# Sliding-window attention: scores as whole 128x128 blocks in place of 32x64 tiles

## The chip, the cores and the metric

The kernel runs on one core of one Trainium2 chip. The metric is the device time of one execution in microseconds (us). The kernel before took 618.32 us as the median of 3 runs (617.77 to 619.11). In the tables and listings PE is TensorE's matmuls, PEld its weight loads, DVE is VectorE, ACT is ScalarE, POOL is GpSimd and SP is SyncE. L490 is line 490 of the kernel before.

## The reference

Two independent problems, A and B, are computed, and their outputs are put side by side. Each is attention with a causal window of 256 keys: S = 2048 tokens, D = 1024, 32 heads of 32, all in bf16.

```python
qkv = (x @ wqkv).reshape(B, S, 3, H, Dh)              # H = 32, Dh = 32
scores = einsum("bhqd,bhkd->bhqk", q, k) * Dh ** -0.5
mask = (idx[:, None] - idx[None, :] >= 0) & (idx[:, None] - idx[None, :] < 256)
scores = where(mask, scores, -1e9)
p = softmax(scores)
o = einsum("bhqk,bhkd->bhqd", p, v)
out = o.transpose(...).reshape(B, S, D) @ wo
```

With blocks of 128 tokens, a block j of keys meets the query blocks j (the diagonal, causal), j + 1 (all of it) and j + 2 (the far edge of the window).

## The kernel before

**Groups and stages.** Four heads make a head group: 4 x 32 = 128 rows. There are 8 groups per problem and 16 in all (G). Each group goes through projections of q and k (transposed, 128 rows by 2048 tokens), scores, exp, masks, accumulation with v, and a norm. v is projected for two groups at once (VG = 2), and the output projection of a problem follows when all its groups are through.

**Scores (`session`, L490 and L497).** Scores are laid out keys by queries. For a key block j the queries are cut in units of 64 (HALF): units 0 and 4 hold halves of the masked diagonal, 1 and 2 the middle block, 3 and 4 the far edge; unit 4 has the upper half of the keys at one end of the window and the lower half at the other. A matmul takes one head (32 rows) and 64 keys, so eight tiles of 32x64 lie beside each other in the array, four heads by two halves of keys. A session takes eight units (SLOTS), 8 x 64 = 512 columns of each of 4 heads, into one fixed tile of four PSUM banks, `scores`. One exp (L497) reads all 2048 columns of it to a bf16 tile `pt`. The 76 units of a group give 16 x 76 / 8 = 152 sessions. The next session's matmuls overwrite the tile, so they wait for the exp. The exp is not shifted by the row maximum; a range check over the inverse row sums (L585) guards it and chooses at the end between this path and a slow one.

**Masks (L507, L518).** GpSimd cuts the triangles out with affine selects of 64 columns: the diagonal goes into a tile `diag` of its own, the far edge is cut in place, 64 or 128 columns at once. Behind each select, `load_piece` may issue one piece of a later weight or x load: a memset of one column on GpSimd, which carries the wait for the buffer, and the DMA on SyncE's queue.

**Accumulation and norm (`edge`, `pv`).** A pair p of query blocks is accumulated PV_LAG = 2 sessions after its last scores. The 128x32 matmuls of L562 put p v into columns 0 to 255 of a PSUM bank `acc` and the row sums, by matmuls with ones, into columns 256 to 383. For the sums, `edge` adds the diagonal and the far block on VectorE first (L529), one session earlier. The norm on VectorE is a reciprocal of the sums (L575), two shuffles (L580), a multiply into `oT` (L582), and for every second pair the range check (L585). `acc` has two buffers, 16 x 8 = 128 pairs use them.

**Projections (`by_columns`, `evacuate`).** A chain is eight matmuls of 512 columns (or 16 of 256) into one of two PSUM banks `pp`, then one cast to bf16. In a session with an accumulation each of the matmuls is issued as four of 128x32 side by side (L199), in others as one of 128x128 (L195). The cast goes to ScalarE (L207) or VectorE (L209).

**What sets the order.** The kernel writes out the order of each engine's instructions by hand, session after session: scores and exp, selects with load pieces, the accumulations that are due, edge adds, then as many projection matmuls as `level` grants. `level` spreads the projections that may run, by the sessions at which their inputs land and at which their outputs are needed, over the sessions that are left, with at most NS_MOST ns each. `_Clock` keeps a running estimate of TensorE, ScalarE and VectorE from constants (COST, ACT_EXP, NS_*). By it `evacuate` picks the engine for a cast, and norms are handed out. An instruction that waits holds up all that stands behind it on its engine; TensorE's order is fixed too.

**Instructions.** Every matmul stands behind a weight load of its own. The program is unrolled, and each engine's instructions come to it by a DMA queue of their own (q8 is TensorE's in the profile).

Of the kernel before, what the change touches and what calls it, by code (L numbers as in the profile page):

```python
# [18 lines left out]
P = 128  # L19
# [7 lines left out]
SLOTS = 8  # L27
HALF = 64
PT_BUFS = 5
DG_BUFS = 4  # L30
VG = 2
NS_MM = 216.0
NS_ROW = 450.0
NS_PV = 52.0
NS_MOST = 3900.0
PV_LAG = 2
# [44 lines left out]
def _fast_path(ctx, tc, cfg, problems, outs, consts, certify):  # L81
# [11 lines left out]
    units = [(j, i) for j in range(NB) for i in range(5)  # L93
             if i in (0, 4) or j + (i + 1) // 2 < NB]
    NE = len(units)
    order = {e: n for n, e in enumerate(units)}
    END = -(-G * NE // SLOTS)

    def parts(j, q):
        return [(j, i) for i in {0: (4, 0), 1: (1, 2), 2: (3, 4)}[q - j]]  # L100

    entries = [(j, q) for j in range(NB) for q in range(j, min(j + 3, NB))]

    def place(g, u):
        return divmod(g * NE + order[u], SLOTS)

    def when(g, j, q, pick=max):
        return pick(place(g, u)[0] for u in parts(j, q))
# [4 lines left out]
    def first_use(g, k, of):  # L113
        return min(when(g, *e, min) for e in entries if e[of] // QB == k)

    def runs(g, us):
        out = []
        for n, u in enumerate(us):
            t, a = place(g, u)
            if out and out[-1][0] == t and out[-1][1] + out[-1][2] == a:  # L120
                out[-1][2] += 1
            else:
                out.append([t, a, 1, n])
        return out
# [8 lines left out]
    ptp = ctx.enter_context(tc.tile_pool(name="pt", bufs=PT_BUFS))  # L133
    diagp = ctx.enter_context(tc.tile_pool(name="diag", bufs=DG_BUFS))
# [9 lines left out]
    edges, diags = {}, {}  # L144
# [149 lines left out]
    def pv_time(g, p):  # L294
        return max(when(g, *e) for e in entries if e[1] // 2 == p) + PV_LAG

# [42 lines left out]
    def units_of(now):  # L339
        return [(n // NE,) + units[n % NE]  # L340
                for n in range(now * SLOTS, min((now + 1) * SLOTS, G * NE))]

    def far_runs(us):
        out = []
        for a, (g, j, i) in enumerate(us):
            if i > 2 and j + 2 < NB:
                if out and i == 4 and out[-1][0] == a - 1:
                    out[-1][1] = 2
                else:
                    out.append([a, 1])  # L350
        return out
# [5 lines left out]
    for time, key, fs in wanted:  # L357
        free = max(free, time)
        new = fs[0]
        for where, f in fs[1:]:  # L360
            while len(pieces.get(free, [])) >= min(2 if key[0] == "x" else 4,
                                                   len(far_runs(units_of(free)))
                                                   + sum(i in (0, 4) for _, _, i in units_of(free))):
                free += 1
            pieces.setdefault(free, []).append((new, where, f))
            new = None
        arrival[key] = free + (3 if key[0] in ("x", "wv") else 2)
# [96 lines left out]

    def session(now):
        us = units_of(now)
        n = len(us)
        clock.pe = max(clock.pe, clock.exp) + NS_ROW
        todo = []
        a = 0  # L470
        while a < n:
            b = a
            while b < n and us[b][:2] == us[a][:2]:
                b += 1
            g, j, _ = us[a]
            lo = [x for x in range(a, b) if us[x][2] < 4]
            hi = [x for x in range(a, b) if us[x][2] < 4 or j + 2 < NB]
            if lo:
                todo.append((g, j, 0, lo[0], len(lo), j * P + HALF * (us[lo[0]][2] + 1)))
            if hi:  # L480
                todo.append((g, j, 1, hi[0], len(hi), j * P + HALF * (us[hi[0]][2] + 1)))
            if us[b - 1][2] == 4:
                todo.append((g, j, 0, b - 1, 1, j * P))
            a = b
        for g, j, c, a, w_, q in todo:
            qT, kT = qks[g]
            keys = slice(j * P + c * HALF, j * P + (c + 1) * HALF)
            for r in range(4):
                rows = slice(32 * r, 32 * r + 32)
                nc.tensor.matmul(  # L490
                    scores[c * HALF:(c + 1) * HALF, r, a * HALF:(a + w_) * HALF],
                    lhsT=kT[rows, keys], rhs=qT[rows, q:q + w_ * HALF],
                    start=True, stop=True, tile_position=(32 * r, c * HALF),
                    skip_group_check=True)
        pt = ptp.tile([P, 4, SLOTS * HALF], BF16, name="pt")
        pts[now] = pt
        nc.scalar.activation(out=pt[:, :, :n * HALF], in_=scores[:, :, :n * HALF],  # L497
                             func=ACT.Exp, bias=-SHIFT, scale=cfg.scale)
        clock.act = max(clock.act, clock.pe) + ACT_EXP
        clock.exp = clock.act  # L500

        def diag(g, j, i):
            p, h = divmod(j, 2)
            if (g, p) not in diags:
                diags[(g, p)] = diagp.tile([P, 4, 2, P], BF16, name="diag")
            lo = HALF if i == 0 else 0
            nc.gpsimd.affine_select(out=diags[(g, p)][:, :, h, lo:lo + HALF],  # L507
                                    in_=pt[:, :, a * HALF:(a + 1) * HALF],
                                    pattern=[[0, 4], [1, HALF]], compare_op=ALU.is_ge, fill=0.0,
                                    base=lo, channel_multiplier=-1)  # L510
            load_piece(now)

        for a, (g, j, i) in enumerate(us):
            if i in (0, 4):
                diag(g, j, i)
        for a, w_ in far_runs(us):
            blk = pt[:, :, a * HALF:(a + w_) * HALF]
            nc.gpsimd.affine_select(out=blk, in_=blk, pattern=[[0, 4], [-1, w_ * HALF]],  # L518
                                    compare_op=ALU.is_gt, fill=0.0,
                                    base=-HALF * (us[a][2] - 3), channel_multiplier=1)  # L520
            load_piece(now)

    def edge(g, p):
        both = edgep.tile([P, 4, 2, P], BF16, name="both")
        dg = diags[(g, p)]
        todo = [(h, n * HALF, w_ * HALF, t, a * HALF) for h in range(2)
                for t, a, w_, n in runs(g, parts(2 * p + h - 2, 2 * p + h))]
        for h, o, w_, t, a in todo:
            nc.vector.tensor_tensor(out=both[:, :, h, o:o + w_], in0=dg[:, :, h, o:o + w_],  # L529
                                    in1=pts[t][:, :, a:a + w_], op=ALU.add)  # L530
            clock.dve = max(clock.dve, clock.pe) + COST["edge"] * (1.0 if w_ == P else 0.65)
        edges[(g, p)] = both

    def pv(g, p):
# [3 lines left out]
        dg = diags.pop((g, p))  # L538

        def old(us):  # L540
            return [(n * HALF, w_ * HALF, pts[s_][:, :, a * HALF:(a + w_) * HALF])
                    for s_, a, w_, n in runs(g, us)]

        mids = [old(parts(q - 1, q)) if q else [] for q in (2 * p, 2 * p + 1)]
        moves = []
        if p:
            moves += [(None, 2 * p - 2) + x for x in old(parts(2 * p - 2, 2 * p))]
            moves += [(None, 2 * p - 1) + x
                      for x in old(parts(2 * p - 1, 2 * p) + parts(2 * p - 1, 2 * p + 1))]
        moves += [(None, 2 * p, P + o, w_, src) for o, w_, src in mids[1]]  # L550
        moves += [(None, 2 * p + i, i * P, P, dg[:, :, i, :]) for i in range(2)]
        for i in range(2):
            moves += [(i, 0, 2 * P + o, w_, src) for o, w_, src in mids[i]]
        acc = ps_acc.tile([P, 512], F32, name="acc")
        clock.pe = max(clock.pe, clock.norms.pop(0))
        sums = edges.pop((g, p)) if p else dg
        moves += [(i, 0, 2 * P, P, sums[:, :, i, :]) for i in range(2)]
        for x, (h, j, o, w_, src) in enumerate(moves):
            for r in range(4):
                c = u * P + 32 * r  # L560
                lhsT = vts[(m, j // QB)][:, j % QB, c:c + 32] if h is None else ones[:, h, :]
                nc.tensor.matmul(acc[32 * r:32 * r + 32, o:o + w_], lhsT=lhsT,  # L562
                                 rhs=src[:, r, :], start=(x == 0), stop=(x == len(moves) - 1),
                                 tile_position=(0, 32 * r), skip_group_check=True)
            clock.pe += NS_PV * w_ / P
# [62 lines left out]
    flips.append(ps_st.tile([P, 4, SLOTS * HALF], F32, name="st")[:, 0])  # L628
# [31 lines left out]
    scores = ps_st.tile([P, 4, SLOTS * HALF], F32, name="st")  # L660
# [241 lines left out]
```

## Time and profile before

The profiled execution took 617.77 us, and its span from first to last recorded instruction is 616.0 us, at a granted TensorE clock of 0.999.

| engine | busy us | share of the span | instructions |
|---|---|---|---|
| PE | 598.9 | 97% | 16665 |
| PEld | 372.8 | 61% | 16665 |
| DVE | 429.9 | 70% | 1143 |
| ACT | 405.8 | 66% | 372 |
| POOL | 372.1 | 60% | 918 |

| group | count | busy us | mean ns of one |
|---|---|---|---|
| L497 exp | 152 | 285.5 | 1878 |
| L207 casts on ACT (512 columns) | 213 | 124.5 | 585 |
| L209 casts on DVE | 42 | 28.3 | 664 to 685 |
| L575 reciprocal | 128 | 121.9 | 953 |
| L529 edge adds | 256 | 144.8 | 602 |
| L580 shuffles | 256 | 64.5 | 297 |
| L582 multiply | 128 | 54.4 | 425 |
| L507 diagonal selects, 64 columns | 512 | 216.3 | 448 |
| L518 far selects | 256 | 161.0 | 647 |

A matmul's own duration is longer than its share of TensorE, since matmuls overlap: what one costs is the distance from its start to the next one's start. Groups whose instructions overlap have a busy time below count times mean. The first scores start at 15.8 us, the last session's at 561.6 us, and from 570.9 us on TensorE runs output projections alone. The DMA engines are busy 80 to 90% of the time in the first two of 40 slices and mostly 0 to 40% later.

### The profile page before, as it was taken

Reading aid. Unit: us, or ns where it says so; the run is one execution under the profiler, and the core shown is the slowest. Engines: PE = TensorE matmul, PEld = TensorE weight load, DVE = VectorE, ACT = ScalarE, POOL = GpSimd, SP = SyncE. Lnnn points to the kernel's source line nnn. Section 1 sums busy time; section 2 is a strip of 40 time slices with the busy share of each in tenths; the row PEclk is TensorE's granted clock in tenths of the full one; section 3 lists DMA queues with packets and bytes.
Section 4 is the critical chain, followed back from the end, with each engine's and each line's share of the span. In section 5 each row is a group of like instructions: output and inputs, shape, how many; then the busy total and the mean of one; then the engine's idle time right before and its main releaser. Section 6 shows DMA issues by size and latency. Waiting matters only on the chain.

```text
span 616.0 us, 36878 instructions
## 1 busy us (share of the span) xinstructions
PE 598.9 (97%) x16665; PEld 372.8 (61%) x16665; DVE 429.9 (70%) x1143; ACT 405.8 (66%) x372; POOL 372.1 (60%) x918
## 2 busy tenths in 40 slices
PE   8999999999999899999999999999999999999996
PEld 4666577657665666656565766756555765555443
DVE  1388878777877678776887757777878778788200
ACT  3667766877776668666676666667766767665332
POOL 0476767776766667675766667566666766665000
PEclk9999999999999999999999999999999999999999
DMA  9814110111024410346011010112021040114221
GB/s 234 176 47 133 37 39 5 39 37 39 5 46 76 95 38 4 67 104 123 29 38 39 4 39 4 39 37 64 29 53 40 5 106 12 56 55 131 70 78 64
DMA packets 86836, 36.00 MB, mean 58 GB/s; under 512 B 65552, under 2 KB 86160, under 8 KB 86672
## 3 DMA queue, kind: packets, MB, share of 16 engines
q1 hardware_dynamic: 85632, 33.31, 22.4%
q8 instruction: 132, 2.16, 1.5%
q10 hardware_dynamic: 1040, 0.26, 0.2%
q14 instruction: 32, 0.26, 0.2%
HBM read 17.83 MB, written 8.39 MB: 43 GB/s over the span
## 4 chain that ended last, share of the span: by engine, by line
PE 90%; issue 3%; POOL 2%; DMA 2%; DVE 1%; ACT 1%; SPq 0%; POOLq 0%; ACTq 0%
PE pp L199 46%; PE pp L195 22%; PE acc L562 13%; PE st L490 9%; DMA xT<-in_A_x_dram 2%; POOL diag L507 1%; POOL pt L518 1%; DVE both L529 0%; DVE rinv L575 0%; ACT pt L497 0%; SPq L603 0%; DVE wide L580 0%; ACT osb L207 0%; DVE top L585 0%; ACT vt L207 0%
## 5 line engine op out<-in xcount | busy, mean ns | idle before, releaser
L497 ACT ACTIVATE pt<-st 128x2048 bf16<-128x2048 f32 x152 | 285.5, 1878 | 90.2 <-PE st L490 63.1
L507 POOL TENSOR_SCALAR_AFFINE_SELECT diag<-pt 128x256 bf16<-128x256 bf16 x512 | 216.3, 448 | 194.3 <-ACT pt L497 180.5
L199 PE MATMUL pp<-xT,wqk 128*32 128x512 bf16 x3092 | 185.9, 379 | 0.4 <-issue 0.4
L575 DVE RECIPROCAL rinv<-acc 128x128 f32<-128x128 f32 x128 | 121.9, 953 | 62.1 <-PE acc L562 61.4
L518 POOL TENSOR_SCALAR_AFFINE_SELECT pt<-pt 128x512 bf16<-128x512 bf16 (+1 forms) x256 | 161.0, 647 | 0.0
L529 DVE TENSOR_TENSOR both<-diag,pt 128x512 bf16<-128x512 bf16 (+1 forms) x256 | 144.8, 602 | 15.1 <-POOL diag L507 11.1
L199 PEld LDWEIGHTS <-wqk 128*32 128x32 bf16 x3092 | 83.1, 97 | 63.3 <-issue 2.0
L199 PE MATMUL pp<-wv,xT 128*32 128x256 bf16 x2840 | 88.4, 273 | 0.5 <-issue 0.5
L199 PEld LDWEIGHTS <-xT 128*32 128x32 bf16 x2840 | 75.5, 97 | 6.6 <-issue 1.1
L490 PEld LDWEIGHTS <-kT 32*64 32x64 bf16 x3904 | 41.1, 103 | 57.6 <-issue 57.4
L490 PE MATMUL st<-qT,kT 32*64 32x64 bf16 (+4 forms) x3904 | 66.3, 236 | 2.3 <-issue 2.2
L580 DVE STREAM_SHUFFLE wide<-rinv 128x128 f32<-128x128 f32 x256 | 64.5, 297 | 0.0
L207 ACT CAST osb<-pp 128x512 bf16<-128x512 f32 (+1 forms) x58 | 33.5, 578 | 46.6 <-PE pp L195 29.3
L195 PE MATMUL pp<-xT,wqk 128*128 128x512 bf16 (+1 forms) x267 | 58.8, 367 | 1.1 <-DMA xT<-in_A_x_dram 1.1
L195 PE MATMUL pp<-wo_sb,oT 128*128 128x512 bf16 (+1 forms) x269 | 58.2, 373 | 0.4 <-ACT vt L207 0.3
L199 PE MATMUL pp<-wo_sb,oT 128*32 128x512 bf16 x1004 | 58.5, 379 | 0.0
L582 DVE TENSOR_TENSOR oT<-acc,wide 128x256 bf16<-128x256 f32 x128 | 54.4, 425 | 4.4
L562 PE MATMUL acc<-pt,vt 128*32 128x128 bf16 (+2 forms) x1792 | 50.8, 224 | 1.5 <-issue 1.4
L562 PEld LDWEIGHTS <-vt 128*32 128x32 bf16 x2816 | 42.4, 96 | 15.8 <-issue 5.2
L207 ACT CAST vt<-pp 128x512 bf16<-128x512 f32 x53 | 30.9, 584 | 20.4 <-PE pp L199 14.1
L207 ACT CAST qT<-pp 128x512 bf16<-128x512 f32 x51 | 29.8, 585 | 21.5 <-PE pp L199 13.8
L195 PEld LDWEIGHTS <-oT 128*128 128x128 bf16 x269 | 25.8, 98 | 29.8 <-issue 0.8
(47 smaller groups left out, 397.3 us busy)
## 6 DMA issues: line engine op xcount, KB each, us to landing
out_dram<-osb SPq DMA_DIRECT2D x63, 128.0 KB, 1.8
wqk<-in_B_wqkv_dram SPq DMA_DIRECT2D x32, 128.0 KB, 3.0
wqk<-in_A_wqkv_dram SPq DMA_DIRECT2D x24, 128.0 KB, 3.5
wo_sb<-in_A_wo_dram SPq DMA_DIRECT2D x16, 128.0 KB, 2.9
wv<-in_B_wqkv_dram SPq DMA_DIRECT2D x16, 128.0 KB, 2.9
wo_sb<-in_B_wo_dram SPq DMA_DIRECT2D x16, 128.0 KB, 2.6
oT<-in_A_x_dram SPq DMA_DIRECT2D x4, 256.0 KB, 5.0
wv<-in_A_wqkv_dram SPq DMA_DIRECT2D x2, 512.0 KB, 4.5
```

What stands on the lines that cost most here:

```text
L195: nc.tensor.matmul(out[:, lo:hi], lhsT=lhsT, rhs=rhs, start=start, stop=stop, skip_group_check=True)
L199: nc.tensor.matmul(out[c:c + 32, lo:hi], lhsT=lhsT[:, c:c + 32], rhs=rhs, start=start, stop=stop, tile_position=(0, c), skip_group_check=True)
L207: nc.scalar.copy(out=out, in_=in_)
L490: nc.tensor.matmul(scores[c * HALF:(c + 1) * HALF, r, a * HALF:(a + w_) * HALF], lhsT=kT[rows, keys], rhs=qT[rows, q:q + w_ * HALF], start ...
L497: nc.scalar.activation(out=pt[:, :, :n * HALF], in_=scores[:, :, :n * HALF], func=ACT.Exp, bias=-SHIFT, scale=cfg.scale)
L507: nc.gpsimd.affine_select(out=diags[(g, p)][:, :, h, lo:lo + HALF], in_=pt[:, :, a * HALF:(a + 1) * HALF], pattern=[[0, 4], [1, HALF]], co ...
L518: nc.gpsimd.affine_select(out=blk, in_=blk, pattern=[[0, 4], [-1, w_ * HALF]], compare_op=ALU.is_gt, fill=0.0, base=-HALF * (us[a][2] - 3) ...
L529: nc.vector.tensor_tensor(out=both[:, :, h, o:o + w_], in0=dg[:, :, h, o:o + w_], in1=pts[t][:, :, a:a + w_], op=ALU.add)
L562: nc.tensor.matmul(acc[32 * r:32 * r + 32, o:o + w_], lhsT=lhsT, rhs=src[:, r, :], start=(x == 0), stop=(x == len(moves) - 1), tile_positi ...
L575: nc.vector.reciprocal(out=inverses[0][:, turn % 2, :], in_=acc[:, 2 * P:3 * P])
L580: nc.vector.stream_shuffle(out=wide[:, h * P:(h + 1) * P], in_=inverses[0][:, turn % 2, :], mask=[16 * h] * 32)
L582: nc.vector.tensor_tensor(out=oTs[(pi, k)][:, t, (p % 2) * 256:(p % 2 + 1) * 256], in0=acc[:, 0:256], in1=wide[:], op=ALU.mult)
```

## The change

Scores are computed for whole blocks of 128 keys by 128 queries with 32x128 tiles (four heads side by side). A session has four such blocks (SLOTS = 4), 45 blocks per group in place of 76 units. The PSUM tile `st` is taken anew from its one-buffer pool in each session. The masks are cut in place in `pt`, one select of 128 columns for a diagonal and one for a far block, and the `diag` tiles are gone. `pt` has 7 buffers instead of 5, and an accumulation follows 3 sessions after its last scores instead of 2. The edge adds and accumulations take whole blocks. The planner's constants change with it (NS_ROW 420, NS_MOST 3300). The range check at L585, which the change's name speaks of, is the same in both kernels.

```diff
-SLOTS = 8
-HALF = 64
-PT_BUFS = 5
-DG_BUFS = 4
+SLOTS = 4
-NS_ROW = 450.0
+NS_ROW = 420.0
-NS_MOST = 3900.0
-PV_LAG = 2
+NS_MOST = 3300.0
+PV_LAG = 3
...
-    units = [(j, i) for j in range(NB) for i in range(5)
-             if i in (0, 4) or j + (i + 1) // 2 < NB]
-    NE = len(units)
+    entries = [(j, q) for j in range(NB) for q in range(j, min(j + 3, NB))]
+    NE = len(entries)
...
-    ptp = ctx.enter_context(tc.tile_pool(name="pt", bufs=PT_BUFS))
-    diagp = ctx.enter_context(tc.tile_pool(name="diag", bufs=DG_BUFS))
+    ptp = ctx.enter_context(tc.tile_pool(name="pt", bufs=7))
...
-        for g, j, c, a, w_, q in todo:
-            qT, kT = qks[g]
-            keys = slice(j * P + c * HALF, j * P + (c + 1) * HALF)
-            for r in range(4):
-                rows = slice(32 * r, 32 * r + 32)
-                nc.tensor.matmul(
-                    scores[c * HALF:(c + 1) * HALF, r, a * HALF:(a + w_) * HALF],
-                    lhsT=kT[rows, keys], rhs=qT[rows, q:q + w_ * HALF],
-                    start=True, stop=True, tile_position=(32 * r, c * HALF),
-                    skip_group_check=True)
+            g, j, q = es[a]
+            qT, kT = qks[g]
+            for r in range(4):
+                nc.tensor.matmul(
+                    st[:, r, a:b, :],
+                    lhsT=kT[32 * r:32 * r + 32, j * P:(j + 1) * P],
+                    rhs=qT[32 * r:32 * r + 32, q * P:(q + b - a) * P],
+                    start=True, stop=True, tile_position=(32 * r, 0))
...
+        for a, (g, j, q) in enumerate(es):
+            blk = pt[:, :, a, :]
+            if q == j:
+                nc.gpsimd.affine_select(out=blk, in_=blk, pattern=[[0, 4], [1, P]],
+                                        compare_op=ALU.is_ge, fill=0.0, base=0,
+                                        channel_multiplier=-1)
+            elif q == j + 2:
+                nc.gpsimd.affine_select(out=blk, in_=blk, pattern=[[0, 4], [-1, P]],
+                                        compare_op=ALU.is_gt, fill=0.0, base=0,
+                                        channel_multiplier=1)
+            if q != j + 1:
+                load_piece(now)
...
+        for h in range(2):
+            (s0, a0), (s1, a1) = (place(g, 2 * p + h - d, 2 * p + h) for d in (0, 2))
+            nc.vector.tensor_tensor(out=both[:, :, h, :], in0=pts[s0][:, :, a0, :],
+                                    in1=pts[s1][:, :, a1, :], op=ALU.add)
+            clock.dve = max(clock.dve, clock.pe) + COST["edge"]
...
-    scores = ps_st.tile([P, 4, SLOTS * HALF], F32, name="st")
```

More of the change, by code (lines that the diff above doesn't have):

```diff
@@ L91, in _fast_path, with place @@
     clock = _Clock()
-    units = [(j, i) for j in range(NB) for i in range(5)
-             if i in (0, 4) or j + (i + 1) // 2 < NB]
-    NE = len(units)
-    order = {e: n for n, e in enumerate(units)}
+    entries = [(j, q) for j in range(NB) for q in range(j, min(j + 3, NB))]
+    NE = len(entries)
+    order = {e: n for n, e in enumerate(entries)}
     END = -(-G * NE // SLOTS)
[L99 to L108, printed above, removed]
+    def place(g, j, q):
+        return divmod(g * NE + order[(j, q)], SLOTS)
     def begin(g):
@@ L113, in first_use @@
     def first_use(g, k, of):
[L114 to L124, printed above, removed]
+        return min(place(g, *e)[0] for e in entries if e[of] // QB == k)
     xpool = ctx.enter_context(tc.tile_pool(name="xT", bufs=NQ + 2))
@@ L143, in _fast_path @@
     xT, wqk, wv, wo_sb, vts, oTs, qks, pts = {}, {}, {}, {}, {}, {}, {}, {}
-    edges, diags = {}, {}
+    edges = {}
     inverses = [None]
@@ L294, in pv_time @@
     def pv_time(g, p):
-        return max(when(g, *e) for e in entries if e[1] // 2 == p) + PV_LAG
+        return max(place(g, *e)[0] for e in entries if e[1] // 2 == p) + PV_LAG
     def wv_time(m):
@@ L337, in _fast_path, with entries_of @@
     wanted.sort(key=lambda w: w[0])
-    def units_of(now):
-        return [(n // NE,) + units[n % NE]
+    def entries_of(now):
+        return [(n // NE,) + entries[n % NE]
                 for n in range(now * SLOTS, min((now + 1) * SLOTS, G * NE))]
[L343 to L351, printed above, removed]
     pieces = {}
@@ L360, in _fast_path @@
         for where, f in fs[1:]:
-            while len(pieces.get(free, [])) >= min(2 if key[0] == "x" else 4,
-                                                   len(far_runs(units_of(free)))
-                                                   + sum(i in (0, 4) for _, _, i in units_of(free))):
+            while len(pieces.get(free, [])) >= min(2 if key[0] == "x" else SLOTS, sum(
+                    q != j + 1 for _, j, q in entries_of(free))):
                 free += 1
@@ L465, in session @@
     def session(now):
-        us = units_of(now)
-        n = len(us)
+        es = entries_of(now)
+        n = len(es)
+        st = ps_st.tile([P, 4, SLOTS, P], F32, name="st")
         clock.pe = max(clock.pe, clock.exp) + NS_ROW
-        todo = []
         a = 0
@@ L472, in session @@
             b = a
-            while b < n and us[b][:2] == us[a][:2]:
+            while b < n and es[b][:2] == es[a][:2]:
                 b += 1
[L475 to L483, printed above, removed]
-            a = b
-        for g, j, c, a, w_, q in todo:
-            qT, kT = qks[g]
-            keys = slice(j * P + c * HALF, j * P + (c + 1) * HALF)
-            for r in range(4):
-                rows = slice(32 * r, 32 * r + 32)
-                nc.tensor.matmul(
-                    scores[c * HALF:(c + 1) * HALF, r, a * HALF:(a + w_) * HALF],
-                    lhsT=kT[rows, keys], rhs=qT[rows, q:q + w_ * HALF],
-                    start=True, stop=True, tile_position=(32 * r, c * HALF),
-                    skip_group_check=True)
-        pt = ptp.tile([P, 4, SLOTS * HALF], BF16, name="pt")
+            g, j, q = es[a]
[6 more added lines that the diff above has]
+                    start=True, stop=True, tile_position=(32 * r, 0))
+            a = b
+        pt = ptp.tile([P, 4, SLOTS, P], BF16, name="pt")
         pts[now] = pt
-        nc.scalar.activation(out=pt[:, :, :n * HALF], in_=scores[:, :, :n * HALF],
+        nc.scalar.activation(out=pt[:, :, :n, :].rearrange("p r a q -> p r (a q)"),
+                             in_=st[:, :, :n, :].rearrange("p r a q -> p r (a q)"),
                              func=ACT.Exp, bias=-SHIFT, scale=cfg.scale)
@@ L500, in session @@
         clock.exp = clock.act
[L502 to L521, printed above, removed]
+        for a, (g, j, q) in enumerate(es):
[10 more added lines that the diff above has]
+                load_piece(now)
@@ L523, in edge @@
     def edge(g, p):
         both = edgep.tile([P, 4, 2, P], BF16, name="both")
[L525 to L531, printed above, removed]
+        for h in range(2):
[3 more added lines that the diff above has]
+            clock.dve = max(clock.dve, clock.pe) + COST["edge"]
@@ L537, in pv @@
         k, h = divmod(p, QB // 2)
[L538 to L553, printed above, removed]
+        segs = []
+        for j in range(max(2 * p - 2, 0), 2 * p + 2):
+            for q in range(max(j, 2 * p), min(j + 3, 2 * p + 2)):
+                s, a = place(g, j, q)
+                if segs and segs[-1][0] == j and segs[-1][2] == s:
+                    segs[-1][4] += 1
+                else:
+                    segs.append([j, q, s, a, 1])
         acc = ps_acc.tile([P, 512], F32, name="acc")
         clock.pe = max(clock.pe, clock.norms.pop(0))
-        sums = edges.pop((g, p)) if p else dg
-        moves += [(i, 0, 2 * P, P, sums[:, :, i, :]) for i in range(2)]
+        moves = [(None, j, (q - 2 * p) * P, n * P, pts[s][:, :, a:a + n, :])
+                 for (j, q, s, a, n) in segs]
+        for (j, q, s, a, n) in segs:
+            for i in range(n):
+                if p == 0 or q + i == j + 1:
+                    moves.append((q + i - 2 * p, j, 2 * P, P, pts[s][:, :, a + i:a + i + 1, :]))
+        if p:
+            both = edges.pop((g, p))
+            moves += [(h, 0, 2 * P, P, both[:, :, h:h + 1, :]) for h in range(2)]
         for x, (h, j, o, w_, src) in enumerate(moves):
@@ L562, in pv @@
                 nc.tensor.matmul(acc[32 * r:32 * r + 32, o:o + w_], lhsT=lhsT,
-                                 rhs=src[:, r, :], start=(x == 0), stop=(x == len(moves) - 1),
+                                 rhs=src[:, r, :, :], start=(x == 0), stop=(x == len(moves) - 1),
                                  tile_position=(0, 32 * r), skip_group_check=True)
@@ L627, in _fast_path @@
     flips = [f[:] for f in flips]
-    flips.append(ps_st.tile([P, 4, SLOTS * HALF], F32, name="st")[:, 0])
+    flips.append(ps_st.tile([P, 4, SLOTS, P], F32, name="st")[:, 0].rearrange("p a q -> p (a q)"))
     flips.append(None)
```

## The prediction

> **What bounds the kernel now.** I read the page first (busy times, queues, chain), then the timeline of TensorE, then the packet records of the instruction queue, and last the groups with shapes kept apart.
>
> ```profile
> span 616.0 us, 36878 instructions
> ...
> PE 598.9 (97%) x16665; PEld 372.8 (61%) x16665; DVE 429.9 (70%) x1143; ACT 405.8 (66%) x372; POOL 372.1 (60%) x918
> ...
> q8 instruction: 132, 2.16, 1.5%
> ...
> PE 90%; issue 3%; POOL 2%; DMA 2%; DVE 1%; ACT 1%; SPq 0%; POOLq 0%; ACTq 0%
> ```
>
> TensorE is busy for 97% and holds 90% of the chain, so the time is TensorE's work plus what TensorE waits for. The "issue" share (3%, in the finer listing 2.6%, 16 us) is waiting for nothing that the profile shows. The timeline shows how such a wait looks:
>
> ```profile
> 207.68 0.43 PE L199 MATMUL pp<-xT,wqk 128*32 128x512 bf16 x4
> 208.04 0.42 PE L490 MATMUL st<-qT,kT 32*64 32x256 bf16 x20
> 208.39 0.40 PE L562 MATMUL acc<-pt,vt 128*32 128x128 bf16 x12
> 208.62 0.28 PE L562 MATMUL acc<-diag,vt 128*32 128x128 bf16 x8
> 208.74 0.28 PE L562 MATMUL acc<-pt,ones 128*32 128x128 bf16 x6
> 209.86 0.23 PE L562 MATMUL acc<-pt,ones 128*32 128x128 bf16 x2 [0.85 <-issue]
> ```
>
> The gap before 209.86 stands in the middle of one accumulation, six matmuls of a group of eight before it and two behind it, where no data can be late. The packet records say what is late: the instruction queue (q8) moves blocks of 16 KB (2.16 MB / 132), and 33,330 TensorE records over some 130 blocks are 256 instructions each. Of the 17 gaps over 0.38 us between 15 and 600 us, 16 stand at the same place of a block (instruction 184 to 190 modulo 256), and each ends 1.2 to 1.6 us after a fetch's packet has ended (206.72 + 1.75 = 208.46, TensorE goes on at 209.86). So TensorE stalls when it runs through a block before the next one is there. The shortest distances between two fetches are 3.2 to 3.5 us: a block that is used up faster than about 3.4 to 3.5 us makes TensorE wait for the rest.
>
> The same start times give the pitches: a 512-column group 216 ns, 256 columns 109, 128 columns 56, 64 columns 29, whether as one 128x128 matmul or four 128x32. Into scores there are 309 instead of 216 ns, so 93 for the change of tile shape. The scores of a session then take 0.35 us to the next line's first matmul (208.04 to 208.39; median 357 ns). A session costs 450 ns. (The planner's constant for it, NS_ROW, is 450 and agrees; the new one is 420.) Adding pitches session by session gives the measured start-to-start within 18 ns each, except in 30 sessions that are 16 us longer together: about 13 us are instruction fetches (below I use 12, the middle of what the block rule gives), some 3 us are waits for projection banks.
>
> **The change, part by part.** The title speaks of a range check, but both kernels read it from the row sums (64 operations at L585, 523 ns, the last line below): that part is nothing. What changes is the score tiling and all that hangs on it.
>
> ```profile
> L497 ACT ACTIVATE pt<-st 128x2048 bf16<-128x2048 f32 x152 | 285.5, 1878 | 90.2 <-PE st L490 63.1 <-issue 10.9 <-PE acc L562 6.6
> ...
> L518 POOL TENSOR_SCALAR_AFFINE_SELECT pt<-pt 128x512 bf16<-128x512 bf16 x192 | 132.0, 698 | 0.0
> L575 DVE RECIPROCAL rinv<-acc 128x128 f32<-128x128 f32 x128 | 121.9, 953 | 62.1 <-PE acc L562 61.4
> L529 DVE TENSOR_TENSOR both<-diag,pt 128x512 bf16<-128x512 bf16 x192 | 113.9, 616 | 14.9 <-POOL diag L507 11.1 <-POOL wqk L377 1.2 <-POOL pt L518 1.1
> ...
> L585 DVE SCALAR_TENSOR_TENSOR top<-rinv,top 128x256 int32<-128x256 int32 x64 | 33.5, 523 | 0.0
> ```
>
> *Scores, +6.7 us.* A head group has 45 blocks of 128x128 in place of 76 units of 64 queries, so 16 groups make 720 / 4 = 180 sessions, not 1216 / 8 = 152. A session streams 512 columns in two or three groups of four 32x128 matmuls, which the trace of before doesn't show. Price: 93 in, about 217 for the columns (163 + 56 or 109 + 109), and 107 out (a 128-column score group to the next line takes 164, a 256-column one 211, against 56 and 109): 417 ns. 180 x 0.417 - 152 x 0.450 = 75.1 - 68.4 = +6.7. Bounds: 400 ns if the wider columns drain faster (-3.1 us from that), 450 ns, the session before, if they cost no less (+5.9). I take 417, next to the constant 420.
>
> *Accumulation, -0.5 us.* By the listed order: 960 groups of 128 columns, 80 of 256, 192 of 64 become 856 of 128 and 180 of 256: 68.0 to 67.6 us. With the 18 ns of 28 more sessions, +0.5, the two cancel.
>
> *Instruction fetch, -10.5 us.* Score matmuls go from 3904 to 1488, accumulating ones from 4928 to 4144, and all matmuls from 16,665 to some 12,840, each with its weight load: 130 blocks become 100. Scores and accumulation together are 132 instructions in 0.95 us before and 81 in 0.95 us after; behind them a projection of 256-column groups, eight instructions in 109 ns, needs 2.4 us for the remaining 175. So the densest block takes about 3.4 us, where it took 2.6. Summing what each block lacks to 3.4 and 3.5 us gives 10.0 and 13.2 us for before, 1.0 and 1.6 us for after. I take 12 to 1.5; bounds 0 and 4 us left.
>
> The Trainium skill (Runtime: NRT & Kernel Launch, section Instruction fetch mechanics) says that the sequencer fetches the next page of 256 instructions while it runs the current one, and that crossing a boundary is mostly hidden. This trace agrees on the size of a block and not on the hiding. By the rule this term would be 0, and the change would come out at 630.8 us.
>
> *Queues of ACT and VectorE, +5.8 us.* 28 more exps of 1.878 us put 53 us on ACT. The planner answers by giving VectorE 79 of the 257 casts instead of 42 (ACT 178 for 215). In the first half the sessions shrink from 3.3 to 2.8 us (planned work divided over more of them). There VectorE has per accumulation 0.95 (reciprocal) + 1.08 (0.875 pairs of edge adds of 616) + 0.50 (two shuffles, 64.5 us over 128) + 0.43 (multiply) + 0.26 (half a range check), and 40 casts for 64 accumulations x 0.67 = 0.42: 3.6 us every 3.98 us, 91%, where 60 to 270 us shows 78%:
>
> ```profile
> 60.00:270.00 210.00, 203.99 (x6362) 134.20 (x6354) 164.28 (x443) 151.09 (x134) 145.64 (x365) 1.00 0.20 42
> ```
>
> Behind a late VectorE stand a cast whose projection bank TensorE needs two chains later (1.73 us per chain), and the norm that frees one of two acc banks. I laid the listed order out with these rows: each exp 0.5 us behind its score start, casts (0.59, 0.67) and norms in their places, TensorE waiting for the bank or the acc two back. For before it gives 3.2 us of waits (the trace leaves 3); for after 9.0, 5.9 for projection banks and 3.0 for acc, the latter between sessions 27 and 81. The exps themselves still fit: 0.56 + 1.88 of 2.8 us. Bounds: 0 more, and twice, +12.
>
> *At nothing.* GpSimd: 768 selects become 480 of 698 ns, 377 to 335 us; VectorE waits 11 us for it in all, and those edge adds are due two sessions later. The 144 load pieces hang on fewer selects and still have two or three sessions, 2 x 2.97 = 5.9 us against landings of 2.6 to 3.5. Without that cover a chain would wait for wqk or wv, a microsecond for each one that a piece is late. At the start x chunk 3 lands at 28.9 us, session 5 begins at 15.8 + 5 x 2.81 = 29.9: 1 us of cover. No queue gets a new DMA. PV_LAG of 3 sessions with 7 pt buffers is 8.9 us for masks and edges, against 7.0 for 2.
>
> **Sum.** +6.7 - 0.5 + 0.5 - 10.5 + 5.8 = +2.0 us on the span of 616.0. The profiled run took 617.77 for that span, the median is 618.32; I add to the median: **620.3 us**. Its own range is 617.5 to 624.
>
> **Rivals.** *The queues hold*: VectorE's backlog stays below the two-bank reserve, since the planner has counted it, and the fetches decide: 620.3 - 5.8 = 614.5 us. For it: ACT and VectorE wait 63 and 61 us for TensorE, and no exp delayed TensorE (the shortest time from an exp's end to the next scores is 0.70 us). Against it: 5% of the chains before already start within 0.05 us of their bank coming free. It decides once the added waits stay under some 2.5 us. *Fetches wait on traffic, not on density*: the fetch at 206.7 took 1.75 us beside the x transposes. Then each fetch costs as before, 12 x 100 / 130 = 9.2 us stay, and 620.3 + 7.7 = 628.0 us, the slower end. Against it: the wait at 393.4 followed a fetch of 0.99 us. *Weight loads of 32x128 show*: one of 98 ns (the 128x128 load) per session, 180 x 0.098 = +17.6, 638 us; but the 32x64 loads of 101 ns follow each other at 3 ns.
>
> **Numbers.** Chances: forecast 0.47, queues hold 0.33, traffic 0.13, weight loads 0.04, the rest 0.03 for a late load. Two runs of this kernel can't be told apart within 0.2%, 1.24 us: faster is below 617.1, slower above 619.6. The rival at 614.5 and a little of the forecast's lower edge give 0.35 faster; most of the forecast and the last three give 0.50 slower; 0.15 between. The range goes from 612 (queues hold and a 400 ns session) to 628.
>
> **What would show it.** Right: 100 q8 blocks and hardly a gap inside an accumulation; scores to next line 0.32 us; VectorE at 85% or more between 60 and 270 us, with TensorE waiting there for casts and for acc. Wrong: gaps at one place of the block as before; sessions far from 417 ns; an even step of 2.8 us in the first half without waits, which is 614.5; or exps that start late and hold the next scores, which I price at 0.1 us.

## The result and the profile after

The changed kernel took 611.24 us (611.07 to 611.60, 4 runs), the kernel before 618.72 us (617.77 to 621.31, 4 runs): a ratio of 0.9873, 95% interval 0.9843 to 0.9904. It is faster where slower was forecast, and it lies 0.8 us below the range. The page of after, with the lines that answer to those shown of before:

```profile
span 609.6 us, 28777 instructions
...
PE 599.8 (98%) x12838; PEld 345.0 (57%) x12838; DVE 437.3 (72%) x1148; ACT 434.8 (71%) x363; POOL 317.8 (52%) x630
...
q8 instruction: 102, 1.67, 1.2%
...
PE 73%; DVE 3%; issue 1%; ACT 1%; DVEq 0%; ACTq 0%
...
L452 ACT ACTIVATE pt<-st 128x2048 bf16<-128x2048 f32 x180 | 338.0, 1878 | 100.0 <-PE st L444 81.3
```

TensorE has 3,827 matmuls fewer: 2,416 of scores, 784 of accumulations and 627 of projections, since fewer of these go as four of 128x32. 102 blocks of instructions are fetched instead of 132. ACT has its 28 more exps at the same 1878 ns. The chain of after can be followed back to 126 us only, so its shares don't compare with those of before. TensorE's own list of waits does (who waited for whom: us in total, times, longest us). Before:

```profile
PE acc L562 <- issue: 4.9, 10, 1.1
PE st L490 <- issue: 2.2, 3, 1.4
PE pp L199 <- issue: 0.9, 2, 0.5
```

After, no line of TensorE's matmuls names issue any more; the longest of those that are left, but for one of 1.3 us at the start that both kernels have, are:

```profile
PE pp L172 <- ACT qT L184: 0.8, 3, 0.4
PE acc L506 <- DVE oT L526: 0.7, 1, 0.7
```

Next TensorE's timeline over one session with an accumulation (start, duration, instruction, count):

```profile
312.28 0.39 PE L176 MATMUL pp<-xT,wqk 128*32 128x512 bf16 x4
312.60 0.40 PE L444 MATMUL st<-qT,kT 32*128 32x384 bf16 x8
312.93 0.51 PE L506 MATMUL acc<-pt,vt 128*32 128x128 bf16 x16
313.27 0.28 PE L506 MATMUL acc<-pt,ones 128*32 128x128 bf16 x8
313.38 0.29 PE L506 MATMUL acc<-both,ones 128*32 128x128 bf16 x8
313.49 2.33 PE L176 MATMUL pp<-xT,wqk 128*32 128x512 bf16 x40
```

Eight score matmuls (twelve in 12 sessions) stand where twenty to thirty-six stood. They take 0.33 us to the next line (0.35 before), and with some 95 ns for the change of shape before them (93 before) the scores of a session cost 423 ns. No gap stands inside an accumulation any more at the place of an instruction block. The gaps that are left look like this one, in the timeline of ACT and TensorE:

```profile
372.52 1.88 ACT L452 ACTIVATE pt<-st 128x2048 bf16<-128x2048 f32 x1 [1.23 <-PE st L444]
372.62 1.91 PE L172 MATMUL pp<-wv,xT 128*128 128x256 bf16 x16
374.29 0.58 ACT L184 CAST kT<-pp 128x512 bf16<-128x512 f32 x1
374.92 0.93 PE L172 MATMUL pp<-wv,xT 128*128 128x256 bf16 x7 [0.39 <-ACT kT L184]
```

A chain ended just behind the start of an exp, its cast had to wait for the exp's 1.88 us on ACT, and TensorE, one chain further, waited for the bank: the queue waits that the prediction speaks of, only fewer. Note that the cast starts at 374.29, before the exp's end at 374.40.

The two spans part into the stretch to the first scores, the sessions and the tail (first scores and last session's scores from TensorE's start times). The second row adds up what the sessions take without a wait: the pitches, that is the distances from start to start by shape, and the few ns by which an undisturbed session exceeds their sum. The third row, called the excess below, is what single sessions take beyond that:

| stretch | before us | after us | difference |
|---|---|---|---|
| to the first scores | 15.8 | 14.0 | -1.8 |
| sessions: sum by pitches and ordinary rest | 530.1 | 537.0 | +6.9 |
| sessions: over that, in single sessions | 15.7 | 4.2 | -11.5 |
| last session's scores to the end | 54.4 | 54.4 | 0.0 |
| span | 616.0 | 609.6 | -6.4 |

The start is one step in the order. Before:

```profile
10.10 2.81 PE L195 MATMUL pp<-xT,wqk 128*128 128x256 bf16 x24
13.98 1.90 PE L195 MATMUL pp<-xT,wqk 128*128 128x512 bf16 x8 [1.08 <-DMA xT<-in_A_x_dram]
15.81 0.42 PE L490 MATMUL st<-qT,kT 32*64 32x256 bf16 x20
```

After:

```profile
12.14 1.91 PE L172 MATMUL pp<-wv,xT 128*128 128x256 bf16 x16
13.98 0.40 PE L444 MATMUL st<-qT,kT 32*128 32x384 bf16 x8
```

Before, the first chain behind the transposes needs x chunk 1, which lands at 13.9 us. With the new sessions that chain is due one session later, so a v chain, which needs chunk 0 alone, comes first and fills the wait.

### The profile page after: what moved, and what is told of

It reads as the page before. It is cut to its first block, busy times and chain, and to the rows that moved or that the text cites. A ratio compares the mean times of both kernels' runs of the same rounds, so it can differ in the third digit from the quotient of the medians.

```text
span 609.6 us, 28777 instructions
## 1 busy us (share of the span) xinstructions
PE 599.8 (98%) x12838; PEld 345.0 (57%) x12838; DVE 437.3 (72%) x1148; ACT 434.8 (71%) x363; POOL 317.8 (52%) x630
## 4 chain that ended last, share of the span: by engine, by line
PE 73%; DVE 3%; issue 1%; ACT 1%; DVEq 0%; ACTq 0%
PE pp L176 34%; PE pp L172 22%; PE acc L506 11%; PE st L444 7%; DVE both L474 1%; DVE rinv L519 1%; DVE wide L524 1%; ACT pt L452 0%; DVE top L529 0%; DVE oT L526 0%; DVE vt L186 0%; ACT qT L184 0%; ACT kT L184 0%; ACT vt L184 0%; ACT osb L184 0%
## 5 line engine op out<-in xcount | busy, mean ns | idle before, releaser
L452 ACT ACTIVATE pt<-st 128x2048 bf16<-128x2048 f32 x180 | 338.0, 1878 | 100.0 <-PE st L444 81.3
L464 POOL TENSOR_SCALAR_AFFINE_SELECT pt<-pt 128x512 bf16<-128x512 bf16 x224 | 149.4, 667 | 153.1 <-ACT pt L452 153.1
L460 POOL TENSOR_SCALAR_AFFINE_SELECT pt<-pt 128x512 bf16<-128x512 bf16 x256 | 175.6, 687 | 88.2 <-ACT pt L452 88.2
L176 PE MATMUL pp<-xT,wqk 128*32 128x512 bf16 x2712 | 163.2, 379 | 0.0
L474 DVE TENSOR_TENSOR both<-pt 128x512 bf16<-128x512 bf16 x224 | 126.5, 605 | 0.8 <-PE acc L506 0.8
L172 PE MATMUL pp<-xT,wqk 128*128 128x512 bf16 (+1 forms) x362 | 82.7, 370 | 0.6 <-ACT qT L184 0.6
L444 PE MATMUL st<-qT,kT 32*128 32x384 bf16 (+2 forms) x1488 | 71.5, 269 | 0.0
L506 PE MATMUL acc<-pt,vt 128*32 128x128 bf16 (+1 forms) x2160 | 63.3, 239 | 0.9 <-DVE oT L526 0.7
L526 DVE TENSOR_TENSOR oT<-acc,wide 128x256 bf16<-128x256 f32 x128 | 54.4, 425 | 4.4
L172 PEld LDWEIGHTS <-wqk 128*128 128x128 bf16 x362 | 33.5, 98 | 36.7 <-issue 6.5
L172 PE MATMUL pp<-wv,xT 128*128 128x256 bf16 x415 | 50.9, 273 | 1.1 <-ACT vt L184 0.5
L172 PEld LDWEIGHTS <-xT 128*128 128x128 bf16 x415 | 39.0, 98 | 11.9 <-issue 5.9
```

What stands on the lines that cost most here:

```text
L172: nc.tensor.matmul(out[:, lo:hi], lhsT=lhsT, rhs=rhs, start=start, stop=stop, skip_group_check=True)
L176: nc.tensor.matmul(out[c:c + 32, lo:hi], lhsT=lhsT[:, c:c + 32], rhs=rhs, start=start, stop=stop, tile_position=(0, c), skip_group_check=True)
L444: nc.tensor.matmul(st[:, r, a:b, :], lhsT=kT[32 * r:32 * r + 32, j * P:(j + 1) * P], rhs=qT[32 * r:32 * r + 32, q * P:(q + b - a) * P], st ...
L452: nc.scalar.activation(out=pt[:, :, :n, :].rearrange("p r a q -> p r (a q)"), in_=st[:, :, :n, :].rearrange("p r a q -> p r (a q)"), func= ...
L474: nc.vector.tensor_tensor(out=both[:, :, h, :], in0=pts[s0][:, :, a0, :], in1=pts[s1][:, :, a1, :], op=ALU.add)
L526: nc.vector.tensor_tensor(out=oTs[(pi, k)][:, t, (p % 2) * 256:(p % 2 + 1) * 256], in0=acc[:, 0:256], in1=wide[:], op=ALU.mult)
```

## The experiments

Two questions stood: whether the 11.5 us are the instruction fetches (theory FETCH) or come from the tiling itself (TILES), and whether queues of ACT and VectorE hold TensorE up as the forecast said (QUEUE), only less. Runs of one job share a chip and the runs of before.

| run | us | before in the same job, us | ratio, 95% interval |
|---|---|---|---|
| b_whole | 615.70 | 616.59 | 0.9966 to 1.0000 |
| a_whole | 624.09 | 616.59 | 1.0091 to 1.0157 |
| a_split | 618.32 | 616.59 | 1.0005 to 1.0050 |
| b_first | 613.76 | 616.59 | 0.9941 to 0.9987 |
| b_stick | 608.13 | 620.46 | 0.9773 to 0.9831 |
| a_c4 | 610.58 | 620.46 | 0.9816 to 0.9869 |
| a_c5 | 628.54 | 620.46 | 1.0103 to 1.0172 |
| after_2 | 611.62 | 615.68 | 0.9913 to 0.9963 |
| b_stick_2 | 607.36 | 615.68 | 0.9847 to 0.9894 |
| b_stick9 | 608.15 | 615.68 | 0.9864 to 0.9913 |

### Fewer instructions in both tilings: b_whole, a_whole

The same edit, once in before and once in after:

```diff
     for now in range(END):
         forced(now)
-        whole[0] = not (due and due[0][0] <= now)
+        whole[0] = True
```

> The kernel before, with every projection issued as one 128x128 matmul, never as four 128x32. TensorE's matmuls fall from 16,665 to about 11,510, blocks of instructions from 130 to 90. Theory FETCH (the gain of the change is that TensorE no longer waits for instruction blocks, some 13 us of before): no gap inside an accumulation or a score session is left, -13 us; 121 more changes of tile shape (accumulation to 128x128) of 95 ns cost +11.4; together about -2 us, near 616.5. Theory TILES (the 32x64 score sessions themselves are dearer than the start times say, fetches are hidden anyway): only the shape changes count, +11.4 us, near 630.

> The same edit in the kernel after: 127 more changes of tile shape, +12 us, near 623 in both theories. What tells them apart is the order of the two tilings with the fetches out of the way. FETCH: the 32x64 kernel with whole projections is now the faster one, by the 7 us that its score work is shorter. TILES: it stays about 7 us slower than this one.

The page of b_whole and its timeline behind an accumulation:

```profile
span 614.0 us, 26571 instructions
...
q8 instruction: 92, 1.51, 1.0%
```

```profile
252.01 0.29 PE L562 MATMUL acc<-pt,ones 128*32 128x128 bf16 x12
252.12 0.29 PE L562 MATMUL acc<-both,ones 128*32 128x128 bf16 x8
252.34 1.90 PE L195 MATMUL pp<-xT,wqk 128*128 128x512 bf16 x8
```

Eight matmuls of 128 columns are two groups, 0.112 us; the projection starts 0.22 us after them, so the change of shape costs 0.11. 121 of these should cost 11 to 13 us. Yet b_whole took 615.70, 0.9 us less than before, since the excess in single sessions fell from 15.7 to 1.1 us. In after, where there was nothing to win, the same edit cost 12.8 us (624.09 against 611.24). And the order flips: without fetch waits the 32x64 tiling is 8.4 us the faster one. TILES had it the slower one by 7. FETCH stands, and with it the price of the new score work.

### More instructions in after: a_split

```diff
-        for c in range(0, P, 32):
-            nc.tensor.matmul(out[c:c + 32, lo:hi], lhsT=lhsT[:, c:c + 32], rhs=rhs, start=start,
-                             stop=stop, tile_position=(0, c), skip_group_check=True)
+        for n in range(0, hi - lo, 256):
+            for c in range(0, P, 32):
+                nc.tensor.matmul(out[c:c + 32, lo + n:lo + n + 256], lhsT=lhsT[:, c:c + 32],
+                                 rhs=rhs[:, n:n + 256], start=start, stop=stop,
+                                 tile_position=(0, c), skip_group_check=True)
```

> The kernel after, with each 128x32 projection matmul of 512 columns cut in two of 256: same columns, 3,660 more matmuls (16,500, 129 blocks, as many as before). FETCH: the gaps at one place of the instruction blocks come back; the block rule with 3.4 to 3.5 us gives 6 to 12 us of them (0.9 to 1.5 without the cut), and the pitch adds 1.9 us: +7 to +13, 618 to 624. TILES: +1.9 us, 613.

This run's output is not the reference's; that the two halves of a projection open their sums in one bank alternately is the likely reason, and it is not shown. The number, shapes and order of TensorE's matmuls are as planned (16,502). The page and one gap of its timeline:

```profile
q8 instruction: 131, 2.15, 1.5%
```

```profile
181.58 0.60 PE L177 MATMUL pp<-xT,wqk 128*32 128x256 bf16 x14
182.34 0.50 PE L177 MATMUL pp<-xT,wqk 128*32 128x256 bf16 x10 [0.16 <-issue]
```

618.32 us is 7.1 over after, at the lower edge of FETCH's 7 to 13 and far from TILES' 1.9. Excess in single sessions rises from 4.2 to 10.1 us in the profile, which is of the slowest of this kernel's ten runs (619.82 us); 0.8 us of it is a wait for an x load at 262.95. The gap shown is in the middle of a group again, 1.5 us after a fetch's packet ended (179.92 + 0.93 = 180.85), with no other wait put down to anything there. So the waits come back with the instructions, with the new tiles in place.

### The first chain: b_first

```diff
-            late = pv_time(VG * m, b // 2) if m or k else 1
+            late = pv_time(VG * m, b // 2) if m or k else min(b, 1)
```

> The kernel before with only the order of the first chain changed, as the listed order of after has it: the first v chain (which needs x chunk 0) before the q chain of x chunk 1. Theory START (part of the gain is that after doesn't wait 1.1 us for chunk 1 ahead of the first scores): first scores at about 14.6 instead of 15.8 us, -1.2 us, near 617.3. Rival: the time is made up for at the next chain that needs chunk 1, or was scatter of the load: 0, near 618.5.

The timeline of TensorE at the start:

```profile
11.79 1.91 PE L195 MATMUL pp<-wv,xT 128*128 128x256 bf16 x16
13.63 0.42 PE L490 MATMUL st<-qT,kT 32*64 32x256 bf16 x20
```

The first scores start 2.2 us earlier, and 2.8 us come off the median (interval 0.8 to 3.6 us of 616.59). START holds; nothing takes it back. It was mis-sized: the old order paid the 1.08 us wait and also had a 1.7 us chain ahead of the scores that could now fill the wait.

### Casts moved between ACT and VectorE: a_c4, a_c5

```diff
-COST = {"act": 590.0, "dve": 670.0, "or": 560.0, "rinv": 930.0, "mult": 900.0,
+COST = {"act": 590.0, "dve": 900.0, "or": 560.0, "rinv": 930.0, "mult": 900.0,
```

(a_c4; a_c5 has 750 and 670.)

> The kernel after, with the planner charging 900 instead of 670 for a cast on VectorE: 51 of 257 casts go there, not 79. Theory QUEUE (TensorE's 4.5 us of single waits in after are casts and norms that come late on ACT and VectorE): laid out in the listed order the waits shrink by a fourth, -1 to -2 us, near 610. Rival (the waits come from elsewhere): 611.2.

> The opposite: the planner charges 750 instead of 590 for a cast on ACT, so VectorE gets 155 casts (104 us of work on it instead of 53). QUEUE: VectorE is full in the first half, norms come late, and TensorE waits for acc banks there: 29 us by the layout that gave 9 for after and 4.5 on the chip, so +11 to +22, 622 to 633. Rival (VectorE has enough slack and bounds nothing): within 1 us of 611.2.

The largest waits of TensorE in a_c5 (who waited for whom: us in total, times, longest us) and its first half (the columns are PE, PEld, DVE, ACT, POOL):

```profile
PE acc L506 <- DVE oT L526: 17.5, 22, 1.7
```

```profile
60.00:270.00 210.00, 200.17 (x4852) 122.12 (x4848) 179.37 (x466) 148.51 (x105) 122.24 (x252) 1.00 0.20 42
```

QUEUE holds where VectorE gets more casts. With 155 casts on VectorE TensorE waits 17.5 us for the norm that frees an acc bank, and the time is 628.54, 17.3 us over after. VectorE is at 85% there (179.37 of 210 us): it holds TensorE up without being full, and its own casts wait some 115 us for TensorE's projections over the whole run. With 51 casts there the time is 610.58, 0.7 us below after: the sign as expected, the size under it, and from two jobs, so I don't call it a gain.

### A version faster than both: b_stick, b_stick_2, b_stick9

The 32x64 tiling with its instructions thinned where they are densest (and the edit of b_first):

```diff
-    def by_columns(out, lo, hi, lhsT, rhs, start, stop):
+    def by_columns(out, lo, hi, lhsT, rhs, start, stop, one=False):
+        whole[0] = whole[0] or one
         if whole[0]:
...
-                               wv[m][:, ct, :], ct == 0, ct == CT - 1)
+                               wv[m][:, ct, :], ct == 0, ct == CT - 1, True)
```

> The 32x64 kernel before, made lighter in instructions where they are densest: in a session with an accumulation, projections go as 128x32 matmuls only until the first v projection (256 columns, eight instructions in 109 ns) and as 128x128 from there; and the v chain goes first at the start. FETCH: 14,155 matmuls, 111 blocks; the block rule leaves 1 us of waits where before has 10 to 13; 57 changes of tile shape cost 5.4 us, the start gives 2.8 back: -12 + 5.4 - 2.8, near 607 beside 616.6 for before, faster than the changed kernel's 611.2, and with little scatter from run to run. Rival (what counts is the tiling, not the blocks): +5.4 - 2.8, near 619.

The page of b_stick:

```profile
span 606.4 us, 31862 instructions
...
PE 598.3 (99%) x14157; PEld 359.2 (59%) x14157; DVE 430.5 (71%) x1143; ACT 405.3 (67%) x372; POOL 372.2 (61%) x918
...
q8 instruction: 112, 1.84, 1.3%
```

It took 608.13 us, 12.3 less than before in the same job, where FETCH had 9.4 less and the rival 2.6 more (before stood higher in this job). The excess in single sessions is 1.7 us. Beside the changed kernel on one chip:

> The changed kernel itself beside the next one on the same chip: near 611.2, scatter under 1 us.

> The 32x64 kernel with whole v projections in the dense sessions and the v chain first, beside the changed kernel on the same chip. FETCH: its work is shorter by 7 - 5.4 = 1.6 us, its queue waits by 2.5 (1.7 against 4.2), fetch waits gone in both: 3 to 4 us below it, near 608. Rival (the 608.1 was the chip's): no difference.

607.36 (606.99 to 607.53) against 611.62 (610.75 to 611.71): 4.3 us, and the two sets of runs don't overlap. In the profiles of these two issue stands against TensorE again, 2.2 and 3.6 us in waits of at most 0.2 us; they are spread over all places of the block, and after_2 stays within 0.4 us of after. With the fetch waits gone from both, the kernel with the old tiling is the faster one: its instructions had held it back.

The last run is b_stick with VectorE's cast charged at 900 in the planner, as in a_c4:

> The same with the planner charging 900 for a cast on VectorE (18 casts there, not 42). QUEUE: ACT has slack (67% busy), so the 1.7 us of waits shrink by up to 1 us, near 607.5. Rival: casts that come late behind an exp on ACT take their place, +1 us or more.

608.15 us, 0.8 above b_stick_2: casts taken from VectorE don't help here. That is the rival's side, near its 1 us, and QUEUE's expectation for this run failed.

## Why the prediction was wrong

**The score work: right, in part by luck.** +6.7 us by a session of 417 ns. Measured are 423 ns, which is 180 x 0.423 - 152 x 0.450 = +7.7 us, and +6.9 with accumulation and the ordinary rest; so these came out 0.8 us cheaper than the 0 of the sum, and the two errors cancel. The weight loads of 32x128 don't show. TensorE has no wait for one of the 180 exps.

**Instruction fetch: right mechanism, too small.** "I take 12 to 1.5", -10.5 us. Of before's 15.7 us of excess only some 1.6 stand elsewhere than behind a fetch, so about 14 are fetches (12.7 if only the waits over 0.06 us are added, 29 of them); after keeps next to none. That is -14, 3.5 us more. The step that failed is the block rule's fixed 3.4 to 3.5 us. From one waiting place to the next the blocks of before that waited 0.19 us or more took 3.2 to 4.6 us, half of them over 3.9. The packet's own time isn't the reason: the two longest waits, 1.6 and 1.3 us, came behind packets of 0.96 us that started 2.2 us after the waiting place before, where the other packets of such blocks started 0.5 to 1.8 us after it. The rule took density alone, and the waits are longest where other queues move data. The share below is that of the DMA engines in the 3 us ahead of the end of the fetch's packet:

| TensorE goes on at, us | wait, us | DMA share |
|---|---|---|
| 104.72 | 0.53 | 0.03 |
| 354.59 | 0.67 | 0.02 |
| 252.48 | 1.64 | 0.73 |
| 393.36 | 1.07 | 0.69 |

15 of the 29 waits, with two thirds of their time, stand beside such traffic, among them all four over 1 us. No run varied the traffic, so its part is seen and not tested. The kernel before also scatters, 613.6 to 622.9 us over all its runs, where after stays within 610.8 to 611.7: the term isn't one number, and the 0.2% within which the prediction held two runs to be alike was too narrow.

**Queues of ACT and VectorE: right mechanism, too large.** +5.8 us forecast (9.0 after against 3.2 before), 2.6 measured (4.2 against 1.6). The step that failed is the layout's allowances. The places are right: the waits stand at casts and at acc, those for acc in sessions 30 to 82 where 27 to 81 were forecast. The sizes are half: some 2.8 us at projection banks for 5.9, and 1.2 at acc for 3.0. By my layout, whose single waits are not shown here, each came out about 250 ns too long: it started an exp 0.5 us behind its scores, a cast only after the exp's end and TensorE 0.08 us behind the cast. The trace has 0.45 us, a cast 0.10 us before that end (the timeline above) and TensorE 0.05 us behind the cast, which makes some 0.2 us of it, where the five longest waits for a bank measure 0.36 to 0.66 us. The 91% of VectorE was no warning either, for it adds durations that overlap. Added in that way, the instructions of 60 to 270 us make 92% after and 86% before; VectorE was busy for 82% there (172.51 of 210 us), against 78% before, and not for the 85% or more that the prediction asked for:

```profile
60.00:270.00 210.00, 208.29 (x5063) 126.31 (x5059) 172.51 (x458) 164.06 (x129) 126.70 (x266) 1.00 0.24 46
```

The sign hung on these two sizes: with 2.6 for the queues the sum was -1.2, with -14 for the fetches -1.5.

**The start: missed.** I priced it at nothing from the landing of chunk 3, and didn't read from the listed order that the first chain changes: -1.8 us in the profiles.

The three errors add to 3.5 + 3.2 + 1.8 = 8.5 us, all the same way; from +2.0 that leads to -6.5, and the spans differ by -6.4. The rival "the queues hold" (614.5 us) was the likelier story in its sign, though its condition, added waits under some 2.5 us, is not clearly met by 2.6; that it left the fetch term and the start as they were is why 611.2 lies below it too. The rival that fetches wait on traffic alone is out: with the same loads the waits went away with the density. The range check runs 64 times in both kernels (33.5 us on VectorE before, 37.0 after) and no wait for it in TensorE's list is over 0.2 us.

Not tried: the old PV_LAG and pt buffers with the new tiles. So what they cost by themselves stays open, as does how much of the 4.3 us between b_stick_2 and after_2 another plan would win back.

## What to carry to other kernels

Count instructions as well as columns: where TensorE runs many short matmuls, divide the listed order into blocks of 256 and ask whether each lasts longer than a fetch (here 3.2 to 4.6 us where TensorE waited); fewer, wider matmuls can win although they stream more columns. When an engine waits for nothing in the middle of a group, look at the place modulo the block and at the instruction queue's packets. And when a sum of terms of both signs ends near zero, the term whose size rests on your own allowances decides: check it against single waits of the trace first.

## What the runs showed of the hardware that was not expected

Instruction fetch gave more than the whole gain: about 14 of 616 us before, most of it in 20 or so waits that each end 1.2 to 1.6 us behind a fetch's packet. It also scatters: kernels with dense blocks (before, b_first, a_split) spread over 3 to 7 us from run to run, most of those without (after, b_whole, a_whole, b_stick_2) over less than 1; b_stick spread over 1.9, and a_c5, which waits for VectorE, over 2.8. And a change from 128x32 to 128x128 matmuls costs about 0.1 us, so some 57 of them were a good price for 20 blocks of instructions less (132 to 112).
